# Splitting w_out on POOL, the first q and k on VectorE, and weight products placed sooner in a fused attention and expert kernel

## The chip, the cores and the metric

The kernel runs on one core of one Trainium2 chip. The metric is device time in microseconds (us), the median of several runs. TensorE is PE, its weight loads PEld, VectorE DVE, ScalarE ACT, GpSimd POOL; SP issues the DMAs.

## What is computed

Attention over 2 batches, 8 heads, 576 positions of width 64, mixed with a memory read; then a gated feed-forward block; then four experts. Cut to what matters:

```python
scores = scale * q @ k.T                 # causal mask, softmax -> a
local = a @ v
q_p = phi(q)                             # elu(q) + 1
mem_out = (q_p @ M_prev) / (q_p @ z_prev + 1e-6)
x = g * mem_out + (1 - g) * local        # 1152 tokens x 512
h = (x @ w1) * (x @ w2) @ w3             # w1, w2: 512 x 1024, w3: 1024 x 1024
x = h @ w_out                            # w_out: 1024 x 512
out = sum_e p[:, e] * (relu(x @ e_w1[e]) @ e_w2[e])   # four experts
```

The weights of the feed-forward block reach the chip as 64-bit floating-point numbers.

## The kernel before, in words

A product of two 32-bit numbers is made of three fast products: each operand is split into a high part (a copy rounded to the type `F32R`) and a low part (the operand less its high part), and the pairs in `PASSES` are summed. So each operand costs one instruction for its high part and one for its low part. `hi_pool` and `lo_pool` run on POOL, `nc.scalar.copy` makes a high part on ACT, `lo_dve` (line 82) a low part on DVE.

The feed-forward weights go through `from64` first: two ACT instructions (lines 101 and 102), then two on DVE (lines 103 and 106) put a 32-bit number together. Its temporary tiles `tf` and `tu` have two buffers each.

Attention works on pairs of heads, eight of them, in slots numbered -1 to 7. In slot n the pair n+2 is loaded and split (`stage_h`), the scores of pair n+1 are made (`stage_a`: products `sc`, a masked minimum by DVE at line 223 out of PSUM, an exponential by ACT at line 230), and pair n is transposed (`pt`, line 257), multiplied by v (`a`, line 270), joined with the memory read (`b`, line 294) and put into `xT`.

Between these steps stand the "fills", PE work that needs no attention result or an older one. `WO_SLOTS` says at which slot each of the eight blocks of w_out is split (`wo_unit`). `W_SLOTS` spreads 16 units that multiply w3 by w_out into `Wt` (`wacc`, line 380; their weights `w3s` are split by POOL). `B_SLOTS` spreads 16 units of x @ w1 and x @ w2 for the first half of the tokens (`ab`, line 432, weights `ws`). `C_SLOTS` spreads eight units of the product with `Wt` (`c`, line 493). The numbers only set the order in which the code is written; a scheduler then orders each engine's instructions. On the chip each engine runs its own list strictly in that order and waits on semaphores.

After attention come the second half of the tokens (again `ab` and `c`) and the experts (lines 600 and 617).

Of the kernel before, what the change touches and what calls it, by code (L numbers as in the profile page):

```python
# [21 lines left out]
T_AT = (0.01, 0.05, 0.09, 0.13, 0.17, 0.21, 0.25, 0.29)  # L22
MEM_AT, PV_AT, JOIN_AT, FIN_AT = 0.11, (0.4, 0.48), 0.54, 0.68

WO_SLOTS = (-0.9, -0.8, -0.7, -0.6, -0.3, -0.1, 0.1, 0.2)
W_SLOTS, B_SLOTS, C_SLOTS = (0.0, 4.0), (4.0, 6.4), (6.4, 8.0)

# [4 lines left out]
def kernel(  # L34
# [17 lines left out]
    nc = tc.nc  # L52
# [19 lines left out]
    def r32(ap):  # L72
        return ap.bitcast(F32)

    def hi_pool(dst, src):
        nc.gpsimd.tensor_scalar(out=dst, in0=src, scalar1=1.0, scalar2=1.0, op0=ALU.mult, op1=ALU.mult)  # L76

    def lo_pool(dst, src, hi):
        nc.gpsimd.tensor_sub(dst, src, r32(hi))  # L79

    def lo_dve(dst, src, hi):
        nc.vector.tensor_sub(dst, src, r32(hi))  # L82
# [10 lines left out]
    def from64(raw, tmp, nm):  # L93

        hi = raw[..., 1]
        shape = list(hi.shape)
        t = tmp.tile(shape, F32, tag="t64f", name=f"tf_{nm}")
        u = tmp.tile(shape, U32, tag="t64u", name=f"tu_{nm}")  # L100
        nc.scalar.activation(u, raw.bitcast(U16)[..., 1], AF.Copy, scale=2.0**-13, bias=2.0**-14 - 0.5)  # L101
        nc.scalar.activation(t, hi.bitcast(F32), AF.Copy, scale=2.0**-112)  # L102
        nc.vector.scalar_tensor_tensor(  # L103
            out=u, in0=t.bitcast(U32), scalar=3, in1=u, op0=ALU.logical_shift_left, op1=ALU.bitwise_or
        )
        nc.vector.scalar_tensor_tensor(  # L106
            out=t.bitcast(U32), in0=hi, scalar=0x80000000, in1=u, op0=ALU.bitwise_and, op1=ALU.bitwise_or
        )
        return t
# [47 lines left out]
    def stage_h(p):  # L157

        if p >= B * H // 2:
            return []  # L160
        qd, kd = raw_t[p]
        qk_t[p] = [A1.tile([P, 2, S], F32R, tag=f"{x}s", name=f"{x}s{p}") for x in "qk"]
        qs, ks = qk_t[p]
        return [
            *zip(
                H_AT,
                (
                    lambda: nc.scalar.copy(qs[:, 0, :], qd),
                    lambda: nc.scalar.copy(ks[:, 0, :], kd),
                    lambda: lo_pool(qs[:, 1, :], qd, qs[:, 0, :]),  # L170
                    lambda: lo_pool(ks[:, 1, :], kd, ks[:, 0, :]),
                ),
            )
        ]
# [149 lines left out]
    def run_slot(n, fill):  # L324
        steps = stage_h(n + 2) + stage_phi(n + 1) + stage_a(n + 1)
        steps += stage_b(n) if n >= 0 else []
        steps += [((i + 0.5) / len(fill), f) for i, f in enumerate(fill)]
        for _, f in sorted(steps, key=lambda t: t[0]):
            f()
# [5 lines left out]
    wo = [po.tile([P, 2, DM], F32R, tag=f"o{c}", name=f"wo{c}") for c in range(KF)]  # L335
# [10 lines left out]
    def wo_load(c):  # L346
        raw_o[c] = r = staging(f"wor{c}").rearrange("p a f two -> p (a f) two")
        nc.sync.dma_start(out=r.rearrange("p n two -> p (n two)"), in_=w_out[c * P : (c + 1) * P, :])

    def wo_unit(c):  # L350
        def f():
            if c + 3 < KF:
                wo_load(c + 3)
            f = from64(raw_o.pop(c), pf, f"wo{c}")
            nc.scalar.copy(wo[c][:, 0, :], f)
            lo_dve(wo[c][:, 1, :], f, wo[c][:, 0, :])
        return f

    NU = 2 * KF
# [28 lines left out]
    def w_unit(u):  # L388
        def pre():
            if u == 0:  # L390
                w_load(0), w_load(1), w_load(2), w_conv(0), w_conv(1)
            if u + 3 < NU:
                w_load(u + 3)

        def post():
            if u + 2 < NU:
                w_conv(u + 2)

        return [pre] + [lambda c=c: w_mm(u, c) for c in range(4)] + [post]
# [67 lines left out]
    for _, f in stage_h(0):  # L467
        f()
# [48 lines left out]
    def spread(slots, units):  # L517
        return [(slots[0] + (slots[1] - slots[0]) * i / len(units), u) for i, u in enumerate(units)]

    fills = [(at, [wo_unit(c)]) for c, at in enumerate(WO_SLOTS)]  # L520
    fills += spread(W_SLOTS, [w_unit(u) for u in range(NU)])
# [152 lines left out]
```

## Time and profile before

| | us |
|---|---|
| median of 3 runs (771.61 to 773.91) | 773.49 |
| the profiled execution | 772.15 |
| its span, first to last instruction | 770.4 |
| PE busy in the span | 743.0 (96%) |
| DVE, ACT, POOL busy | 299.5, 252.6, 246.1 |

A busy share says how long an engine had an instruction under way. PE is the engine that nearly fills the span, so the question for any edit is which of the 27 us in which PE has nothing under way it can give back, and whether PE's own instructions take the same time before and after. An instruction's idle time in front of it stands in square brackets with what released it.

### The profile page before, as it was taken

The numbers are of one execution on the slowest core, as the hardware profiler recorded it, in microseconds if no ns is written. First come the engines' busy times: TensorE is split into PE (matmuls) and PEld (weight loads), VectorE is DVE, ScalarE is ACT, GpSimd is POOL, SyncE is SP. The second block draws the span as 40 slices with busy tenths as digits, with TensorE's granted clock in tenths as the row PEclk, the third lists the DMA queues.
The fourth block names the chain that finished last, engine by engine and source line by source line (L and its number), as shares of the span: only waits on it lengthen the run. The fifth ranks groups of instructions, "written<-read, shape, count | busy, mean of one in ns | idle before, by whom it ended". The sixth has DMA issues, their size and how long they took to land.

```text
span 770.4 us, 11304 instructions
## 1 busy us (share of the span) xinstructions
PE 743.0 (96%) x4568; PEld 656.0 (85%) x4568; DVE 299.5 (39%) x642; ACT 252.6 (33%) x503; POOL 246.1 (32%) x244
## 2 busy tenths in 40 slices
PE   4899999999999998999999999999999999999997
PEld 2778888898888998999889898898988899888986
DVE  6967656667666225653312121212212122121221
ACT  7966556555556324542201011011111011010100
POOL 2164553444351029332940069000492003400000
PEclk9999999999999999999999999999999999999999
DMA  9773412332422015420420024000141000101010
GB/s 273 252 209 110 130 47 70 97 89 84 126 83 83 2 54 163 127 83 2 138 82 1 1 67 127 26 1 1 50 129 42 1 1 27 42 1 53 3 42 28
DMA packets 52596, 56.69 MB, mean 74 GB/s; under 512 B 15552, under 2 KB 40128, under 8 KB 52544
## 3 DMA queue, kind: packets, MB, share of 16 engines
q1 hardware_dynamic: 52544, 55.97, 24.1%
q8 instruction: 36, 0.59, 0.3%
q14 instruction: 16, 0.13, 0.1%
HBM read 53.60 MB, written 2.36 MB: 73 GB/s over the span
## 4 chain that ended last, share of the span: by engine, by line
PE 63%; DMA 2%; DVE 1%; POOL 1%; ACT 1%; issue 0%; DVEq 0%; SPq 0%; ACTq 0%
PE d L600 26%; PE o L617 26%; PE c L493 6%; PE ab L432 3%; DMA wr<-in_moe_w_dram 2%; PE a L270 1%; DVE tu L103 0%; POOL ws L79 0%; DVE tf L106 0%; PE pt L257 0%; POOL el L76 0%; POOL el L79 0%; DVE hT L82 0%; ACT tu L101 0%; ACT tf L102 0%
## 5 line engine op out<-in xcount | busy, mean ns | idle before, releaser
L617 PE MATMUL o<-el,he 128*128 128x512 f32 x864 | 201.3, 393 | 0.0
L617 PEld LDWEIGHTS o<-el,he 128*128 128x128 f32 x864 | 161.8, 188 | 36.6
L606 ACT ACTIVATE he<-d 128x512 fp32r<-128x512 f32 (+2 forms) x96 | 47.2, 491 | 342.4 <-PE d L600 339.9
L432 PE MATMUL ab<-xT,ws 128*128 128x288 f32 x768 | 113.1, 299 | 7.2 <-DVE asb L480 3.2
L600 PE MATMUL d<-x2b,el 128*128 128x384 f32 (+1 forms) x768 | 113.7, 308 | 0.0
L600 PEld LDWEIGHTS d<-x2b,el 128*128 128x128 f32 x768 | 113.1, 189 | 0.7
L432 PEld LDWEIGHTS ab<-xT,ws 128*128 128x128 f32 x768 | 103.9, 188 | 10.2 <-DVE asb L480 3.3
L607 DVE SCALAR_TENSOR_TENSOR he<-d,he 128x512 fp32r<-128x512 f32 (+2 forms) x96 | 53.5, 557 | 147.8 <-ACT he L606 147.8
L76 POOL TENSOR_SCALAR el<-rel 128x512 fp32r<-128x512 f32 x64 | 40.1, 632 | 216.3 <-PE d L600 187.2
L600 PE MATMUL d<-x2a,el 128*128 128x512 f32 x384 | 89.6, 394 | 0.0
L600 PEld LDWEIGHTS d<-x2a,el 128*128 128x128 f32 x384 | 72.0, 188 | 16.8
L79 POOL TENSOR_TENSOR el<-rel,el 128x512 fp32r<-128x512 f32 x64 | 83.1, 1313 | 1.6
L626 DVE SCALAR_TENSOR_TENSOR acc<-o,pr,acc 128x512 f32<-128x512 f32 x27 | 20.3, 751 | 125.7 <-PE o L617 125.7
L270 PEld LDWEIGHTS a<-v,pT 114*120 114x120 f32 (+1 forms) x480 | 55.4, 193 | 3.9 <-issue 2.6
L493 PE MATMUL c<-hT,W 128*128 128x288 f32 x384 | 57.6, 299 | 1.0 <-DVE hT L82 0.8
L270 PE MATMUL a<-v,pT 114*120 114x65 f32 (+1 forms) x480 | 56.7, 276 | 0.4 <-DVE mn L223 0.4
L79 POOL TENSOR_TENSOR ws<-tf,ws 128x512 fp32r<-128x512 f32 x32 | 44.9, 1402 | 38.2 <-ACT ws L422 36.9
L493 PEld LDWEIGHTS c<-hT,W 128*128 128x128 f32 x384 | 52.3, 188 | 2.6 <-DVE hT L82 1.5
L380 PE MATMUL wacc<-wo,w3s 128*128 128x512 f32 x192 | 49.9, 408 | 0.0
L217 PE MATMUL sc<-ks,qs 64*120 64x120 f32 (+5 forms) x288 | 37.2, 375 | 12.5 <-POOL ks L79 9.3
L230 ACT ACTIVATE P<-P,mn 120x120 f32<-120x120 f32 (+3 forms) x80 | 42.4, 578 | 2.0 <-DVE mn L223 1.8
L380 PEld LDWEIGHTS wacc<-wo,w3s 128*128 128x128 f32 x192 | 35.9, 194 | 7.6 <-issue 0.7
(75 smaller groups left out, 634.9 us busy)
## 6 DMA issues: line engine op xcount, KB each, us to landing
wr<-in_moe_w_dram SPq DMA_DIRECT2D x32, 512.0 KB, 3.6
rel<-in_moe_w_dram SPq DMA_DIRECT2D x64, 256.0 KB, 2.7
w3r<-in_moe_w3T_dram SPq DMA_DIRECT2D x16, 512.0 KB, 3.9
wor<-in_moe_w_out_dram SPq DMA_DIRECT2D x8, 512.0 KB, 6.7
v<-in_v_dram SPq DMA_DIRECT2D x16, 150.0 KB, 4.0
qd<-in_qT_dram SPq DMA_DIRECT2D x8, 288.0 KB, 3.3
kd<-in_kT_dram SPq DMA_DIRECT2D x8, 288.0 KB, 3.5
out_dram<-acc SPq DMA_DIRECT2D x9, 256.0 KB, 2.0
```

The costliest lines, as they stand in the source:

```text
L76: nc.gpsimd.tensor_scalar(out=dst, in0=src, scalar1=1.0, scalar2=1.0, op0=ALU.mult, op1=ALU.mult)
L79: nc.gpsimd.tensor_sub(dst, src, r32(hi))
L217: nc.tensor.matmul(ps[x][:, c : c + k1 - k0], lhsT=qs[o, a, q0[i] : q0[i] + RP], rhs=ks[o, b, k0:k1], start=(m == 0), stop=(m == 2),)
L230: nc.scalar.activation(Pt[i], Pt[i], AF.Exp, bias=mn[:, i : i + 1], scale=-1.0)
L270: nc.tensor.matmul(st["a"][:, x, i, :], lhsT=pt[x, i, j][0 : rows[j]], rhs=vn[0 : rows[j], j, :], start=(j == 0), stop=(j == i),)
L380: nc.tensor.matmul(wacc[t], lhsT=w3s[u][:, a, c, :], rhs=wo[4 * g + c][:, bb, :], start=(g == 0 and c == 0 and x == 0), stop=(g == 1 and c ...
L432: nc.tensor.matmul(ps[:, 0:HS], lhsT=self.ws[u][:, wi, kk, :], rhs=xT[b, kk][:, xi, a * HS : (a + 1) * HS], start=(n == 0), stop=(n == 3 * ...
L493: nc.tensor.matmul(st["ps"][:, 0:HS], lhsT=Wt[kk][:, wi, d * P : (d + 1) * P], rhs=hT[kk][:, xi, a * HS : (a + 1) * HS], start=(kk == 0 an ...
L600: nc.tensor.matmul(ps, lhsT=ew1[m // 4 * 4 + kk][:, wi, m % 4 * P : (m % 4 + 1) * P], rhs=rhs[:, xi, :], start=(n == 0), stop=(n == 3 * KD ...
L606: nc.scalar.activation(ht[:, 0, :], ps, AF.Relu)
L607: nc.vector.scalar_tensor_tensor(out=ht[:, 1, :], in0=ps, scalar=0.0, in1=r32(ht[:, 0, :]), op0=ALU.max, op1=ALU.subtract,)
L617: nc.tensor.matmul(po, lhsT=hs[kk][:, xi, tt * P : (tt + 1) * P], rhs=ew2[kk][:, wi, :], start=(n == 0), stop=(n == 3 * KF - 1),)
```

## The change

It does three things. The high and low parts of the eight w_out blocks are made by POOL; before, ACT made the high and DVE the low part. The low parts of q and k of the first pair (only that pair) are made by DVE; before, by POOL. And the slots move: the w_out blocks now all lie in slot -1, the w3 units start 0.2 slots sooner, the first `ab` units 0.2 sooner and over 2.5 slots where there were 2.4, the `c` units 0.1 sooner and over 1.7.

```diff
-WO_SLOTS = (-0.9, -0.8, -0.7, -0.6, -0.3, -0.1, 0.1, 0.2)
-W_SLOTS, B_SLOTS, C_SLOTS = (0.0, 4.0), (4.0, 6.4), (6.4, 8.0)
+WO_SLOTS = (-0.95, -0.85, -0.75, -0.65, -0.5, -0.35, -0.2, -0.1)
+W_SLOTS, B_SLOTS, C_SLOTS = (-0.2, 3.8), (3.8, 6.3), (6.3, 8.0)
...
+        lo = lo_pool if p else lo_dve
...
-                    lambda: lo_pool(qs[:, 1, :], qd, qs[:, 0, :]),
-                    lambda: lo_pool(ks[:, 1, :], kd, ks[:, 0, :]),
+                    lambda: lo(qs[:, 1, :], qd, qs[:, 0, :]),
+                    lambda: lo(ks[:, 1, :], kd, ks[:, 0, :]),
...
-            nc.scalar.copy(wo[c][:, 0, :], f)
-            lo_dve(wo[c][:, 1, :], f, wo[c][:, 0, :])
+            hi_pool(wo[c][:, 0, :], f)
+            lo_pool(wo[c][:, 1, :], f, wo[c][:, 0, :])
```

POOL's list from its first split on, before (`qs` and `ks` are the split q and k, 138 and 139 the first pair, 154 and 155 the second; `w3s` is a split w3 unit):

```order
L79 TENSOR_TENSOR qs_138<-qd_122,qs_138 128x576
L79 TENSOR_TENSOR ks_139<-kd_124,ks_139 128x576
L79 TENSOR_TENSOR qs_154<-qd_148,qs_154 128x576
L79 TENSOR_TENSOR ks_155<-kd_150,ks_155 128x576
L76 TENSOR_SCALAR w3s_369<-tf_l_363 128x512
L79 TENSOR_TENSOR w3s_369<-tf_l_363,w3s_369 128x512
```

The same place now (`wo_114` is the first split w_out block, `wo_121`, further down, the last):

```order
L76 TENSOR_SCALAR wo_114<-tf_wo_172 128x512
L79 TENSOR_TENSOR wo_114<-tf_wo_172,wo_114 128x512
L76 TENSOR_SCALAR wo_115<-tf_wo_182 128x512
L79 TENSOR_TENSOR wo_115<-tf_wo_182,wo_115 128x512
L76 TENSOR_SCALAR wo_116<-tf_wo_192 128x512
L79 TENSOR_TENSOR wo_116<-tf_wo_192,wo_116 128x512
L76 TENSOR_SCALAR wo_117<-tf_wo_223 128x512
L79 TENSOR_TENSOR wo_117<-tf_wo_223,wo_117 128x512
L79 TENSOR_TENSOR qs_154<-qd_148,qs_154 128x576
L79 TENSOR_TENSOR ks_155<-kd_150,ks_155 128x576
```

Four w_out blocks stand ahead of the second pair's q and k, and the other four between these and the first w3 unit: 16 POOL instructions more in front of the first `w3s`.

DVE's list from its third instruction on, before:

```order
L188 TENSOR_SCALAR ex_156<-ex_156 128x576
L189 SCALAR_TENSOR_TENSOR phi_157<-qd_122,ex_156 128x576
L103 SCALAR_TENSOR_TENSOR tu_wo_173<-tf_wo_172,tu_wo_173 128x512
L106 SCALAR_TENSOR_TENSOR tf_wo_172<-wor_130,tu_wo_173 128x512
L103 SCALAR_TENSOR_TENSOR tu_wo_204<-tf_wo_203,tu_wo_204 128x512
L82 TENSOR_TENSOR wo_114<-tf_wo_172,wo_114 128x512
L106 SCALAR_TENSOR_TENSOR tf_wo_203<-wor_132,tu_wo_204 128x512
```

And now:

```order
L82 TENSOR_TENSOR qs_138<-qd_122,qs_138 128x576
L189 TENSOR_SCALAR ex_156<-ex_156 128x576
L82 TENSOR_TENSOR ks_139<-kd_124,ks_139 128x576
L190 SCALAR_TENSOR_TENSOR phi_157<-qd_122,ex_156 128x576
L103 SCALAR_TENSOR_TENSOR tu_wo_173<-tf_wo_172,tu_wo_173 128x512
L106 SCALAR_TENSOR_TENSOR tf_wo_172<-wor_130,tu_wo_173 128x512
L103 SCALAR_TENSOR_TENSOR tu_wo_183<-tf_wo_182,tu_wo_183 128x512
```

The low parts of the first q and k have come in, and the low part of the first w_out block is gone (so are the other seven further down).

POOL's list early in the second half of the tokens, before (`el` is a split expert weight, `ws_2` the third split unit of w1 and w2 of that half):

```order
L76 TENSOR_SCALAR el_0_1_3873<-rel_0_1_3871 128x512
L76 TENSOR_SCALAR el_0_2_3878<-rel_0_2_3876 128x512
L79 TENSOR_TENSOR el_0_1_3873<-rel_0_1_3871,el_0_1_3873 128x512
L79 TENSOR_TENSOR el_0_2_3878<-rel_0_2_3876,el_0_2_3878 128x512
L79 TENSOR_TENSOR ws_2_3261<-tf_2_3255,ws_2_3261 128x512
```

And now:

```order
L76 TENSOR_SCALAR el_0_1_3873<-rel_0_1_3871 128x512
L76 TENSOR_SCALAR el_0_2_3878<-rel_0_2_3876 128x512
L79 TENSOR_TENSOR el_0_1_3873<-rel_0_1_3871,el_0_1_3873 128x512
L79 TENSOR_TENSOR ws_2_3261<-tf_2_3255,ws_2_3261 128x512
L79 TENSOR_TENSOR el_0_2_3878<-rel_0_2_3876,el_0_2_3878 128x512
```

The low part of `ws_2` has changed places with that of an expert weight.

## Rows read from the trace of the kernel before

**Rows 1.** Stretches: start:end, length, busy PE, PEld, DVE, ACT, POOL, clock, DMA

```profile
8.61:40.12 31.51, 25.80 (x145) 20.81 (x145) 30.18 (x82) 28.79 (x56) 4.98 (x4) 1.00 0.89 269
...
146.00:250.00 104.00, 98.83 (x810) 91.39 (x809) 68.59 (x167) 61.15 (x127) 41.35 (x37) 1.00 0.31 93
284.00:360.00 76.00, 72.34 (x529) 70.25 (x528) 38.36 (x60) 34.89 (x72) 36.35 (x30) 1.00 0.34 104
```

**Rows 2.** Timeline, first microseconds: start us, us, engine line op tiles [idle before]

```profile
5.98 0.66 ACT L169 CAST ks<-kd 128x576 fp32r<-128x576 f32 x1
...
6.93 1.62 POOL L79 TENSOR_TENSOR ks<-kd,ks 128x576 fp32r<-128x576 f32 x1
...
7.32 1.85 DVE L189 SCALAR_TENSOR_TENSOR phi<-qd,ex 128x576 f32<-128x576 f32 x1
...
8.61 2.88 PE L217 MATMUL sc<-ks,qs 64*120 64x120 f32 x24 [8.61 <-POOL ks L79]
```

**Rows 3.** Timeline of PE, around its first products with weights

```profile
33.28 4.66 PE L270 MATMUL a<-v,pT 114*120 114x65 f32 x22 [0.41 <-DVE mn L223]
...
40.12 0.77 PE L380 MATMUL wacc<-wo,w3s 128*128 128x512 f32 x1
...
42.26 4.17 PE L380 MATMUL wacc<-wo,w3s 128*128 128x512 f32 x12
...
54.88 5.72 PE L380 MATMUL wacc<-wo,w3s 128*128 128x512 f32 x24
```

**Rows 4.** Timeline of DVE and POOL, the last steps before the first weight product

```profile
37.04 0.68 DVE L106 SCALAR_TENSOR_TENSOR tf_l<-w3r,tu_l 128x512 uint32<-128x512 uint32 x1
...
38.51 1.58 POOL L79 TENSOR_TENSOR w3s<-tf_l,w3s 128x512 fp32r<-128x512 f32 x1
```

**Rows 5.** Groups of DVE, 10 to 38 us: count | busy us, mean ns | idle before

```profile
L82 DVE TENSOR_TENSOR wo<-tf_wo,wo 128x512 fp32r<-128x512 f32 x8 | 6.9, 860 | 0.5 <-ACT wo L355 0.4
L106 DVE SCALAR_TENSOR_TENSOR tf_wo<-wor,tu_wo 128x512 uint32<-128x512 uint32 x8 | 5.5, 685 | 0.1
L103 DVE SCALAR_TENSOR_TENSOR tu_wo<-tf_wo,tu_wo 128x512 uint32<-128x512 uint32 x7 | 4.8, 681 | 0.0
```

**Rows 6.** Groups of POOL, 36 to 75 us

```profile
L79 POOL TENSOR_TENSOR w3s<-tf_l,w3s 128x512 fp32r<-128x512 f32 x8 | 11.2, 1398 | 0.7
L76 POOL TENSOR_SCALAR w3s<-tf_l 128x512 fp32r<-128x512 f32 x8 | 5.5, 683 | 28.4 <-DVE tf_l L106 15.6 <-PE wacc L380 12.8
```

**Rows 7.** Timeline, DVE instructions that meet a POOL instruction

```profile
22.20 1.41 POOL L79 TENSOR_TENSOR ks<-kd,ks 128x576 fp32r<-128x576 f32 x1
...
22.33 1.82 DVE L82 TENSOR_TENSOR wo<-tf_wo,wo 128x512 fp32r<-128x512 f32 x1 [0.17 <-ACT wo L355]
...
47.00 1.30 POOL L79 TENSOR_TENSOR w3s<-tf_l,w3s 128x512 fp32r<-128x512 f32 x1
...
47.13 0.75 DVE L223 CUSTOM_DVE_ANT_0 P<-sc,mask,mn 120x512 f32<-120x512 f32 x1 [0.77 <-PE sc L217]
```

**Rows 8.** Groups of DVE, 38 to 110 us, where POOL splits w3 units

```profile
L103 DVE SCALAR_TENSOR_TENSOR tu_l<-tf_l,tu_l 128x512 uint32<-128x512 uint32 x13 | 11.5, 887 | 12.4 <-ACT tf_l L102 12.4
L106 DVE SCALAR_TENSOR_TENSOR tf_l<-w3r,tu_l 128x512 uint32<-128x512 uint32 x13 | 10.0, 771 | 0.8
...
L82 DVE TENSOR_TENSOR xT<-x,xT 128x576 fp32r<-128x576 f32 x2 | 1.5, 744 | 0.0
```

**Rows 9.** Timeline, two of PE's later waits and what stands before them

```profile
212.39 1.82 PE L432 MATMUL ab<-xT,ws 128*128 128x288 f32 x12 [1.95 <-POOL ks L79]
...
289.70 0.62 ACT L422 CAST ws<-tf 128x512 fp32r<-128x512 f32 x1 [0.60 <-PE ab L432]
...
290.73 1.54 POOL L79 TENSOR_TENSOR ws<-tf,ws 128x512 fp32r<-128x512 f32 x1
...
292.32 3.19 PE L432 MATMUL ab<-xT,ws 128*128 128x288 f32 x22 [1.71 <-POOL ws L79]
```

## The prediction, made before the changed kernel ran

> **What bounds the kernel now.** I read the busy time by stretch first and looked for PE's idle time. It has nothing under way for 8.61 us until its first product [rows 2], for 31.51 - 25.80 = 5.71 us from there to its first weight product at 40.12, for 104.00 - 98.83 = 5.17 between 146 and 250, and for 76.00 - 72.34 = 3.66 between 284 and 360 [rows 1]. With the last 4 us, in which DVE and a DMA finish after PE, that is all of the 27 us. From 360 on there is nothing that the change could hide better.
>
> Next I read how fast PE runs. The clock column says 1.00 in all these stretches, so I go by durations: 22 `a` products take 4.66 us at 33.28; 12 `wacc` products 4.17 us at 42.26, but 24 of the same only 5.72 us (0.238 each) at 54.88 [rows 3]. If the slow ones take twice that, 4.17 us are some 5.5 slow ones and 6.5 fast ones, which puts the change of pace at 42.26 + 2.6 = 44.9. So PE runs at its lower level, 1.2 GHz, for the first 45 us and at 2.4 GHz after. What stands ahead of the first weight product, 25.80 us of work, is done at the low level in both kernels, and what counts is when the weight products can start. I call that moment T; before, T = 40.12.
>
> What sets T is DVE. In 8.61 to 40.12 it is busy for 30.18 of 31.51 us, POOL for 4.98 [rows 1]. DVE's line 106 ends the first w3 unit at 37.72, POOL's low part of it ends at 40.09, and PE's first `wacc` starts at 40.12 [rows 3, 4].
>
> **Part by part.** *First q and k.* POOL's low part of k ends at 8.55 and PE starts at 8.61; ACT had its high part ready at 6.64 [rows 2]. DVE needs 0.74 us for one of that size [rows 8]: q at 5.6, ex at 6.3, k from 6.72 to 7.47, so PE starts at 7.5, 1.1 us sooner. phi, which took 1.85 us beside POOL's work and ended at 9.17 [rows 2], then takes 0.74 too and ends at 8.2, so DVE reaches the w_out blocks 0.9 us sooner. This is worth something only if DVE keeps its lead until T.
>
> *What leaves DVE and ACT.* Eight copies leave ACT, and eight low parts, 6.9 us in sum [rows 5], leave DVE; seven of these (some 5.9 us) stand in front of the first w3 unit. With DVE's list otherwise the same, line 106 would end at 37.72 - 0.9 - 5.9 = 30.9 and T be 33.3. PE can't be ready sooner either: 7.5 + 25.8 = 33.3. That is the best case.
>
> *What comes to POOL.* Eight times 0.68 + 1.40 us [rows 6], 16.6 us, with the second pair's q and k (2 x 1.4, [rows 7]) in the middle. From 9.6 on this ends at 29.0 if POOL never waits, so POOL's length alone isn't the bound. But DVE waits for POOL. The low part at 22.33 took 1.82 us where line 103 of like size takes 0.68, and it ended 0.54 us after POOL's instruction of 22.20 had ended; the minimum out of PSUM at 47.13 met a POOL instruction as well and took 0.75, no more than the 0.74 above [rows 5, 7, 8]. So a DVE instruction with both inputs in SBUF doesn't run beside one of POOL's, and one out of PSUM does. The Trainium skill, page "SBUF — State Buffer", section "Who interferes with whom", says the same: DVE with two SBUF inputs and a POOL instruction that reads SBUF shut each other out, and whoever comes second waits. By that rule the best case can't be had, and offering work to POOL isn't free.
>
> The price of that. DVE has 21 such instructions between 9.5 us and the end of line 106 for the first w3 unit (8 of line 103, 8 of 106, 3 of ex, 2 of phi). From below: where POOL splits w3 units now, line 103 takes 0.21 us more than here and line 106 0.09 [rows 5, 8]; 0.15 each for 21 is 3.1, so T = 36.4. From above: I walked DVE's and POOL's new lists side by side from 8.2 us, with these durations, DVE's PSUM work (5 us a pair) running beside POOL, and each clash going to whoever was there first. Twelve waits come out, 0.1 to 1.2 us, 7.6 in sum; the largest lie behind the second pair's q and k (1.2), the sixth block (1.1) and the eighth (0.8). DVE also waits a little for ACT, which can't refill a temporary tile before POOL has read it. Line 106 then ends at 39.6, and POOL, held up by DVE in turn, ends the first unit at 42.4. I take T = 41, nearer the walk, since in the stretch of rows 8 POOL rests about half the time, and here it has a queue.
>
> *From T on.* All of the first head's `a` products now stand ahead of T (0.45 us of them came after it), so the end moves by 41 - 40.12 - 0.45 = +0.4. The pace changed 4.8 us after T, with the same work in between; I keep that, with 2 us either way, worth 1 us, since work at the low level takes twice as long. The second block of `wacc` needs two units that POOL makes behind the third pair's q and k: in the walk they are there at 54.3 and needed at 56, so this costs nothing; with POOL 2 us later it would cost 0.5.
>
> *Slots.* Between 45 and 146 us PE is full already, so products that come sooner find no idle time there. In 146 to 250 the 5.17 us are mostly waits of `ab` for a PSUM buffer that ACT or DVE empties late; the largest is 1.95 at 212.39 [rows 9]. It is put down to POOL's split of k, which these products don't read; the copies they need stood on ACT behind q, k and two exponentials. The new list spreads the 16 units over 4% more time and gives each such place other neighbours. A gain or loss of up to 2 us is open; I take 0. SP's list changes by one or two places, with loads of w3 and w1 ahead of a q or k that they followed; I cost that at nothing, since the loads run ahead of their use by a slot.
>
> *After attention.* PE waits 1.71 us at 292.32 for a low part that POOL began at 290.73, behind expert weights; its high part was ready at 290.32 [rows 9]. With the two changed about it can start 0.4 us sooner: -0.4.
>
> **Sum.** On the profiled execution 772.15 + 0.4 + 0 - 0.4 = 772.2. The median of the runs lies 1.34 above that execution, so 773.5.
>
> **Rivals.** *DVE and POOL seldom meet.* With T = 37 the end moves by -3.6 - 0.4: 769.5. For it: the small excess of rows 8. Against: POOL's queue is full here. Chance 0.25.
>
> *DVE waits as in the walk, and longer (the side of slower).* The place is DVE's list between 20 and 42 us. Each wait there also holds up the minimum behind it, for which PE's next scores wait, and line 106, for which POOL's next block waits. It decides from T = 43 on, where the shift is +2.4; at 43.7, with 0.5 at the second block of `wacc`, it gives 776.7. Chance 0.22.
>
> *The slots decide.* If the new neighbours clear the 5.17 us [rows 1] the time is 768.3, if they add half as much 776.1; 0.04 each.
>
> *The clock comes sooner.* PE had hardly a gap from 33.7 to 44.9 and stayed at the low level until the `wacc` stream [rows 3], so the rows speak against it. The work between T and the change of pace, 4.8 us, done at the high level gives back 2.4: 771.1, on the edge of no change; 0.03. The Trainium skill, page "TensorE: Matmul & The Clock Gate", says in its first part that the low clock is the default and sustained activity releases it. The trace bears that out for the `wacc` stream, and not for the small products ahead of it.
>
> **Numbers.** A measurement of this kernel can tell 0.3%, 2.3 us, from no change. No change has 0.45 (the forecast 0.42, the sooner clock 0.03); faster 0.25 + 0.04; slower 0.22 + 0.04. T from 36.4 to 44.5 with the slots' 2 us and the clock's 1 us reaches from 766 to 781; without the outer fifth, 768.5 to 778.
>
> **What would show it.** In the new profile: PE's first product near 7.5; DVE's lines 103 and 106 before 40 us at 0.9 to 1.1 us in the mean (0.68 if they don't meet POOL); the first `wacc` near 41 with PE idle for some 4 us in front of it; the change of pace 3 to 7 us later; 3 to 7 us of waits between 146 and 250; the wait near 292 at 1.3. The forecast is wrong if T lies below 38.5 or above 43, or if the stretch 146 to 250 gains or loses more than 2 us.

## The result, and the profile after

| | median us | runs |
|---|---|---|
| before | 772.07 | 6 (771.38 to 773.91) |
| changed | 778.74 | 6 (777.63 to 780.79) |

The ratio is 1.0086, 95% interval 1.007 to 1.0102: the change makes the kernel slower by 6.7 us. The forecast was no change, 773.5 us in a range of 768.5 to 778. The profiled execution of the changed kernel took 777.63 us, 5.48 more than that of before.

From line 164 on every line number is one higher than before (one line was added). The stretches of the changed kernel, to hold against [rows 1] (columns as there):

```profile
7.49:40.61 33.12, 23.77 (x147) 18.62 (x147) 30.98 (x73) 27.48 (x52) 22.01 (x19) 0.94 0.89 271
40.61:61.00 20.39, 16.86 (x75) 13.31 (x76) 11.70 (x20) 9.99 (x16) 10.80 (x10) 0.76 0.57 164
...
286.00:364.00 78.00, 73.17 (x536) 70.92 (x535) 41.92 (x60) 36.51 (x77) 37.50 (x30) 1.00 0.33 105
```

PE has nothing under way for 33.12 - 23.77 = 9.35 us between its first product and its first weight product, where it was 5.71, and for another 3.53 us in the 20 us behind it. The clock column (1.00 is 2.4 GHz, 0.50 is 1.2 GHz) needs care: ahead of the first rise in the records it shows 1.00 for the lower level too. So in [rows 1] it said 1.00 for a stretch that ran at 1.2 GHz; here it is under 1 because the clock rose at 29.7 us, fell at 36.5, rose at 46.8, fell at 57.0 and rose for good at 60.4. Before, it rose once, at 44.7.

The timeline of PE in the changed kernel, its larger waits up to 60 us (start, length, instruction, idle time ahead and what ended it), to hold against [rows 2, 3]:

```profile
7.49 2.88 PE L218 MATMUL sc<-ks,qs 64*120 64x120 f32 x24 [7.49 <-DVE ks L82]
...
25.68 1.55 PE L218 MATMUL sc<-ks,qs 64*120 64x120 f32 x12 [1.67 <-POOL ks L79]
...
34.58 4.51 PE L271 MATMUL a<-v,pT 114*120 114x65 f32 x30 [2.74 <-DVE mn L224]
40.61 0.79 PE L381 MATMUL wacc<-wo,w3s 128*128 128x512 f32 x1 [1.52 <-POOL w3s L76]
...
53.21 0.78 PE L258 MATMUL pt<-identF,P 120*120 120x120 f32 x6
57.52 0.77 PE L381 MATMUL wacc<-wo,w3s 128*128 128x512 f32 x1 [3.53 <-DVE W L82]
```

The first product stands at 7.49 and the first weight product at 40.61, where the forecast had 7.5 and 41. The last line is new: the second block of `wacc` waits 3.53 us. It is released by VectorE's low part of `W`, which is made out of the accumulator of the first block. That accumulator is the same PSUM buffer (tag M1, one buffer), so no product of the second block can start before `W` has been made from it, although the first block's last product ended at 50.5.

Why `W` came so late stands in the timelines of POOL, ACT and DVE of the changed kernel (in this order, not by time):

```profile
49.58 1.42 POOL L79 TENSOR_TENSOR qs<-qd,qs 128x576 fp32r<-128x576 f32 x1 [3.56 <-ACT qs L169]
50.95 1.41 POOL L79 TENSOR_TENSOR ks<-kd,ks 128x576 fp32r<-128x576 f32 x1
52.32 0.62 POOL L76 TENSOR_SCALAR w3s<-tf_l 128x512 fp32r<-128x512 f32 x1
53.03 1.27 POOL L79 TENSOR_TENSOR w3s<-tf_l,w3s 128x512 fp32r<-128x512 f32 x1
54.27 0.62 POOL L76 TENSOR_SCALAR w3s<-tf_l 128x512 fp32r<-128x512 f32 x1
54.97 1.26 POOL L79 TENSOR_TENSOR w3s<-tf_l,w3s 128x512 fp32r<-128x512 f32 x1
...
54.33 0.67 ACT L102 ACTIVATE tf_l<-w3r 128x512 f32<-128x512 f32 x1 [2.91 <-POOL w3s L79]
54.91 0.57 ACT L386 CAST W<-wacc 128x512 fp32r<-128x512 f32 x1
...
55.03 1.75 DVE L103 SCALAR_TENSOR_TENSOR tu_l<-tf_l,tu_l 128x512 uint32<-128x512 uint32 x1 [5.46 <-ACT tf_l L102]
56.70 0.68 DVE L82 TENSOR_TENSOR W<-wacc,W 128x512 fp32r<-128x512 f32 x1
```

Read it from the end. VectorE's `W` stands behind line 103, which took 1.75 us beside POOL's instruction of 54.97 (it ended 0.55 us after it) and had waited 5.46 us for ACT. ACT's copy of the accumulator stands behind line 102, which waited 2.91 us for a temporary tile `tf` (two buffers) to be read by POOL. POOL read it last at 53.03, because ahead of it stood q and k of the third pair, and POOL sat idle for 3.56 us until ACT had made their high parts. Nobody here needed q and k of the third pair yet (PE's first scores from them start at 73.24); they only stood in the list. Before, POOL's third unit of w3 stood ahead of them, at 47.00 [rows 7].

To account for the whole 5.48 us I add up PE's time in the two traces: its first product -1.12; waits from there to 64 us +6.87 (6.02 to 12.89); waits from 64 to 284 us -2.83 (5.17 to 2.34); waits behind that +1.17 (3.66 to 4.83); the products themselves +1.39 (743.05 to 744.43). The products can be split further. PE's busy time at the lower level (before the first rise, and wherever the records say 0.5) was 30.43 us and is 28.77. My estimate is that half of it would go at the upper level; that is 15.2 and 14.4 us, so 0.8 came back there, and the rest of the busy time grew by 2.2 us, from 727.8 to 730.0.

### The profile page after: what moved, and what is told of

It is laid out like the page before. It is cut to its first block, busy times and chain, and to the rows that moved or that the text cites. A ratio compares the mean times of both kernels' runs of the same rounds, so it can differ in the third digit from the quotient of the medians.

```text
span 775.8 us, 11324 instructions
## 1 busy us (share of the span) xinstructions
PE 744.4 (96%) x4568; PEld 655.3 (84%) x4568; DVE 300.5 (39%) x636; ACT 252.3 (33%) x495; POOL 263.7 (34%) x258
## 4 chain that ended last, share of the span: by engine, by line
PE 62%; DMA 3%; POOL 2%; DVE 2%; ACT 2%; issue 1%; DVEq 0%; POOLq 0%; SPq 0%; ACTq 0%
PE d L601 26%; PE o L618 26%; PE c L494 5%; PE ab L433 3%; DMA wr<-in_moe_w_dram 3%; PE a L271 2%; POOL el L79 1%; POOL ws L79 1%; DVE tf L106 1%; POOL el L76 1%; PE pt L258 1%; ACT tu L101 1%; PE sc L218 0%; DVE tu L103 0%; ACT tf L102 0%
## 5 line engine op out<-in xcount | busy, mean ns | idle before, releaser
L381 PE MATMUL wacc<-wo,w3s 128*128 128x512 f32 x192 | 54.5, 426 | 5.5 <-DVE W L82 4.0
L271 PEld LDWEIGHTS a<-v,pT 114*120 114x120 f32 (+1 forms) x480 | 53.7, 188 | 5.2 <-DVE mn L224 3.0
L271 PE MATMUL a<-v,pT 114*120 114x65 f32 (+1 forms) x480 | 54.6, 270 | 2.7 <-DVE mn L224 2.7
L381 PEld LDWEIGHTS wacc<-wo,w3s 128*128 128x128 f32 x192 | 36.8, 201 | 14.9 <-issue 5.9
```

What stands on the lines that cost most here:

```text
L271: nc.tensor.matmul(st["a"][:, x, i, :], lhsT=pt[x, i, j][0 : rows[j]], rhs=vn[0 : rows[j], j, :], start=(j == 0), stop=(j == i),)
L381: nc.tensor.matmul(wacc[t], lhsT=w3s[u][:, a, c, :], rhs=wo[4 * g + c][:, bb, :], start=(g == 0 and c == 0 and x == 0), stop=(g == 1 and c ...
```

## The experiments

The change has three parts: **S**, the slots; **O**, w_out on POOL; **Q**, the first pair's q and k on VectorE. All eight settings were run, and then variants. Each time is a median, with the kernel before run on the same chip in the same job. The columns after the ratio come from each kernel's profiled execution, by the sum above: first product, waits to 64, from 64 to 284 and behind 284 us, half of the busy time at the lower level (an estimate of what that level costs), and all other busy time.

| run | what it has | median, before | ratio (95%) | first | waits | half low | other |
|---|---|---|---|---|---|---|---|
| before | | | | 8.61 | 6.0, 5.2, 3.7 | 15.2 | 727.8 |
| the change | S O Q | 778.74, 772.07 | 1.007 to 1.010 | 7.49 | 12.9, 2.3, 4.8 | 14.4 | 730.0 |
| after_again | S O Q | 780.84, 771.95 | 1.0075 to 1.013 | 7.41 | 11.4, 4.5, 4.1 | 18.7 | 729.9 |
| slots_only | S | 771.16, 771.64 | 0.998 to 1.001 | 8.58 | 7.7, 2.1, 4.4 | 12.7 | 730.0 |
| wo_pool_only | O | 774.86, 771.64 | 1.002 to 1.005 | 8.56 | 8.5, 3.4, 4.1 | 15.6 | 728.5 |
| qk_dve_only | Q | 771.89, 771.64 | 0.999 to 1.002 | 7.47 | 7.7, 3.9, 2.9 | 16.5 | 727.0 |
| slots_qk | S Q | 776.09, 771.64 | 1.004 to 1.008 | 7.47 | 5.8, 3.7, 4.4 | 18.6 | 729.4 |
| slots_wo | S O | 778.61, 771.95 | 1.005 to 1.010 | 8.57 | 10.2, 3.2, 4.5 | 14.9 | 730.9 |
| qk_wo | O Q | 778.36, 771.95 | 1.005 to 1.009 | 7.48 | 13.0, 3.5, 3.9 | 17.4 | 727.5 |

The change and after_again are the same kernel, and their profiled executions differ by 1.5, 2.2 and 0.7 us in the three columns of waits and by 4.3 us in the lower level. So one execution's difference of that size says little by itself.

**The slots alone** (slots_only). Edit:

```diff
-WO_SLOTS = (-0.9, -0.8, -0.7, -0.6, -0.3, -0.1, 0.1, 0.2)
-W_SLOTS, B_SLOTS, C_SLOTS = (0.0, 4.0), (4.0, 6.4), (6.4, 8.0)
+WO_SLOTS = (-0.95, -0.85, -0.75, -0.65, -0.5, -0.35, -0.2, -0.1)
+W_SLOTS, B_SLOTS, C_SLOTS = (-0.2, 3.8), (3.8, 6.3), (6.3, 8.0)
```

> The kernel before with only the three rows of slots changed (w_out's units and the products with weights 0.2 of a pair sooner); w_out's parts stay on ScalarE and VectorE, the first pair's low parts of q and k on GpSimd. Theory A (the loss comes from w_out's parts on GpSimd, which make GpSimd late and hold up ScalarE): no wait of more than 1 us ahead of the second block of products w3 with w_out; the waits between 146 and 250 us fall from 5.2 to about 1.3 us, the ones after 284 us grow by 1.2 us: 772.1 - 3.9 + 1.2, so 769.4 us, 768 to 771. Rival B (the slots themselves put the second block too soon after the first): a wait of 3 to 4 us ahead of the second block here too, and a time of 776 to 778.5 us.

Measured 771.16 us, no difference from before and just above theory A's bracket. The second block waited 1.87 us, between the two theories. The waits between 64 and 284 us did fall by 3.1 us, yet the time did not, and the trace says where that went. One line each for before, this kernel and the one with w_out on POOL alone, from the end of the second `wacc` block to the same product `c` at the end of attention (the 192nd), columns as in [rows 1]:

```profile
60.60:283.00 222.40, 217.22 (x1730) 195.90 (x1729) 131.78 (x337) 122.10 (x245) 83.05 (x73) 1.00 0.27 78
```

```profile
59.53:280.87 221.34, 219.34 (x1738) 197.02 (x1736) 128.41 (x336) 124.55 (x243) 84.56 (x73) 1.00 0.27 79
```

```profile
64.17:284.78 220.61, 217.18 (x1730) 195.89 (x1729) 130.03 (x337) 122.68 (x245) 82.65 (x73) 1.00 0.27 78
```

With the old slots PE is busy 217.2 us there, with the new ones 219.3 (220.2 in the changed kernel). Seven more transposes lie in the stretch, 0.6 us; the other 1.5 is the same products at the same clock. This is no chance of one execution: cut in the same way, qk_dve_only, qk_wo and before_qkall, with the old slots, lie within 0.1 us of before, and the other kernels with the new ones and no added products have 3.0 to 4.5 us more than before (in slots_qk and slots_wo the clock fell once in the stretch). Counted in the traces, `wacc` products and attention's change places more often (165 changes from one kind of product to another became 178), and a block that is broken up takes longer: before, 24 `wacc` in a row took 5.72 us [rows 3], 15 and 9 of them 3.68 + 2.31. So the new slots fill PE's waits, and PE's own products take back most of what that gives. That the finer mixing is the reason fits these counts; no run tested it alone.

**w_out on POOL alone** (wo_pool_only). Edit:

```diff
-            nc.scalar.copy(wo[c][:, 0, :], f)
-            lo_dve(wo[c][:, 1, :], f, wo[c][:, 0, :])
+            hi_pool(wo[c][:, 0, :], f)
+            lo_pool(wo[c][:, 1, :], f, wo[c][:, 0, :])
```

> The kernel before with only w_out's high and low parts moved to GpSimd; slots and q, k as before. Theory A: the second block of products w3 with w_out waits 2 to 5 us, for an accumulator that is emptied late or for a part of w_out, TensorE's clock comes later or falls once more, and nothing is given back between 146 and 250 us (5.2 us of waits as before): 777 to 782 us, above the changed kernel's 778.7 more likely than below. Rival B: within 1.5 us of the kernel before, 771 to 773.5 us, since the slots stand as before.

Measured 774.86 us, 3.2 above before: under theory A's bracket and over rival B's. No wait stood ahead of its second block; it lost 2.5 us in waits before 64 us, one of them for q and k of the second pair behind w_out on POOL (2.79 us at 28.0).

**The first q and k alone** (qk_dve_only). Edit:

```diff
+        lo = lo_pool if p else lo_dve
...
-                    lambda: lo_pool(qs[:, 1, :], qd, qs[:, 0, :]),
-                    lambda: lo_pool(ks[:, 1, :], kd, ks[:, 0, :]),
+                    lambda: lo(qs[:, 1, :], qd, qs[:, 0, :]),
+                    lambda: lo(ks[:, 1, :], kd, ks[:, 0, :]),
```

> The kernel before with only the first pair's low parts of q and k moved from GpSimd to VectorE. Both theories: the first product comes 1.1 us sooner (near 7.5 us), the start of the products with weights is set by VectorE and not by q and k, so at most this 1.1 us is kept and at worst VectorE is as much later: 771 to 772.8 us, waits after 61 us as before.

Measured 771.89 us, as expected. The first product came 1.1 us sooner and nothing of it was left.

**Slots with q and k** (slots_qk; the first and third edit).

> The changed kernel with w_out's parts put back on ScalarE and VectorE: slots and the first pair's q and k as changed. Theory A: 768 to 771 us, faster than the kernel before, no wait over 1 us ahead of the second block, and about 1.3 us of waits between 146 and 250 us. Rival B: the wait of 3 to 4 us ahead of the second block stays, 775 to 778.5 us. Rival C (the fallen clock is the loss, and the wait only its sign): the clock is granted in full from the first block on in this kernel if its products run without a wait, and the 24 products of the second block take 5.7 us rather than 7.1.

Measured 776.09 us. Theory A fails here: with w_out off POOL the kernel is still 4.5 us slower than before, though no wait over 0.45 us stands between 33 and 87 us. Rival B has the time but not its wait. What the trace shows instead is the clock. The same 22 `a` products in slots_only and in slots_qk, on PE's timeline:

```profile
33.26 2.52 PE L270 MATMUL a<-v,pT 114*120 114x65 f32 x22 [0.51 <-DVE mn L223]
```

```profile
33.07 4.66 PE L271 MATMUL a<-v,pT 114*120 114x65 f32 x22 [0.45 <-DVE mn L224]
```

In slots_only the clock had risen at 32.5 us (it fell again at 35.9 and rose for good at 42.8); in slots_qk it rose at 47.0. In the table that is 18.6 against 12.7 us, more than the whole difference of the two profiled executions (775.04 and 771.20). Part of it comes much later: PE waited 1.92 us for VectorE ahead of 183.53, the clock was lower from 183.6 to 187.0, and 12 `ab` products took 3.24 us there where the next 12 took 1.85. Of rival C's sign half is there, without a gain: the second block's 24 products take 5.73 us, but the first block began at the lower level. All 9 runs of slots_qk (774.0 to 778.3) lie above all 12 of slots_only (770.0 to 773.0), but a clock record exists for one execution of each, so that the clock explains all the runs is not shown.

**The two other pairs** (slots_wo, qk_wo; the first and second, the second and third edit), with the change once more beside them (after_again).

> The changed kernel as it is, once more, on the chip of the next three: 777.5 to 779.5 us, with about 3.5 us of wait ahead of the second block of products w3 with w_out, behind GpSimd, ScalarE and VectorE in this order.

> The changed kernel with the first pair's low parts of q and k back on GpSimd: slots and w_out as changed. By the sum of the parts measured alone (slots -0.5 us, w_out on GpSimd +3.2 us) 774.3 us. Theory A (w_out on GpSimd and the sooner slots together make the wait ahead of the second block): 776 to 779 us, with 3 us or more of wait there. Rival D (the sooner q and k together with the slots are what costs, 4.7 us more in that pair than the two alone): 773.5 to 775 us.

> The changed kernel with the slots back as before: w_out on GpSimd and the first pair's q and k on VectorE. By the sum of the parts measured alone (+3.2 and +0.25 us) 775.1 us; theories A and D both 774 to 776 us, with less than 1.5 us of wait ahead of the second block and 3.4 us or more of waits between 61 and 284 us. Above 777 us, neither holds: q and k with w_out would then be a pair that costs by itself.

The change measured 780.84 us, above its bracket, with 4.22 us of wait ahead of the second block. slots_wo had theory A's time, 778.61, without its wait: its waits stand ahead of the first block, and its second block runs at 57.3 without one. Two of them on PE's timeline, for POOL and for VectorE:

```profile
28.04 1.55 PE L217 MATMUL sc<-ks,qs 64*120 64x120 f32 x12 [2.79 <-POOL ks L79]
...
36.47 1.68 PE L270 MATMUL a<-v,pT 114*120 114x65 f32 x14 [1.85 <-DVE mn L223]
```

qk_wo, 778.36, lies above what either theory allowed, and with the old slots shows the chain of the changed kernel once more. From its timelines of ACT, DVE and PE:

```profile
54.23 0.67 ACT L102 ACTIVATE tf_l<-w3r 128x512 f32<-128x512 f32 x1 [2.91 <-POOL w3s L79]
...
58.81 0.68 DVE L82 TENSOR_TENSOR W<-wacc,W 128x512 fp32r<-128x512 f32 x1
...
59.14 1.65 PE L258 MATMUL pt<-identF,P 120*120 120x120 f32 x7 [5.88 <-ACT pT L260]
```

So that chain doesn't need the new slots. ACT waits 2.91 us for POOL as in the changed kernel, and PE 5.88 us for a copy that ACT makes behind it.

Over the eight settings w_out on POOL costs 3.2 us (old slots, old q and k), 7.1 (new slots), 6.2 (new q and k), and 2.2 to 4.4 (both; by the two jobs that ran the change). It is the one part that costs in every setting. The three don't add. From the first weight product to the end of the second block of `wacc` the four kernels with w_out on POOL take 22.2 to 27.9 us, before 20.5, and the other three settings 19.2 to 21.9. But only the change and qk_wo show the chain of ACT's 2.91 us there; what w_out on POOL costs in wo_pool_only and slots_wo is not explained by it.

**The cause taken away** (after_p2dve). The changed kernel with q and k of the third pair on VectorE, which stood idle for 5.46 us just there. The lists of ACT and PE stay as they are:

```diff
-        lo = lo_pool if p else lo_dve
+        lo = lo_dve if p in (0, 2) else lo_pool
```

> The changed kernel with one more edit: the low parts of q and k of the third pair are made by VectorE too, which stood idle from 49.6 to 55.0 us, and no longer by GpSimd ahead of the third and fourth unit of w3. The orders of ScalarE and of TensorE stay as they are. Theory A (the accumulator of the second block is emptied late because ScalarE and VectorE stand behind GpSimd's q and k of the third pair): GpSimd's third unit ends near 48 instead of 54.3 us, the accumulator is empty near 53.5 instead of 57.4 us, the wait of 3.5 us ahead of the second block falls under 0.6 us, the clock does not fall there, and the time comes down by 3 to 5 us, to 774 to 776 us. Rival E (the clock and the finer mixing of products are the loss, the wait is made up later): less than 1 us is gained, 778 to 779 us.

Measured 775.67 us against 780.84 for the change in the same job: 5.2 us gained, and inside theory A's 774 to 776. (The change had only 4 runs there. By the first measurement, 6.7 us over before against 3.7 here, it is 3.0.) The same places in its timelines (POOL, ACT, DVE, PE):

```profile
49.47 1.30 POOL L79 TENSOR_TENSOR w3s<-tf_l,w3s 128x512 fp32r<-128x512 f32 x1
...
52.56 0.59 ACT L386 CAST W<-wacc 128x512 fp32r<-128x512 f32 x1
...
50.22 1.16 DVE L82 TENSOR_TENSOR qs<-qd,qs 128x576 fp32r<-128x576 f32 x1
51.30 0.75 DVE L82 TENSOR_TENSOR ks<-kd,ks 128x576 fp32r<-128x576 f32 x1
...
54.36 0.68 DVE L82 TENSOR_TENSOR W<-wacc,W 128x512 fp32r<-128x512 f32 x1
...
55.18 1.17 PE L381 MATMUL wacc<-wo,w3s 128*128 128x512 f32 x4 [0.35 <-DVE W L82]
```

POOL's third unit of w3 ends at 50.8 instead of 54.3, ACT's line 102 waits for nothing, and the wait ahead of the second block is 0.35 us. The clock rose for good at 47.9 and didn't fall again. From the first weight product to the end of the second block, where the edit acts, this kernel takes 19.6 us, the change 24.0 (24.9 in after_again) and before 20.5. The sum of waits to 64 us shows less of it (11.4 to 10.0), because in this execution more wait, 9.7 us for 7.1, stood ahead of that product. 3.7 us over before remain. By the sum they are wait ahead of the first weight product (9.7 us, before 5.7) and other busy time (+2.7), less what the lower level costs (-2.3).

**All q and k on VectorE** (before_qkall, slots_qkall, after_qkall: the kernel before, slots_qk and the change, with `lo = lo_dve` for every pair).

> The kernel before with the low parts of q and k of all eight pairs made by VectorE (14 more than in the run with the first pair alone): GpSimd is rid of 16 subtractions of 1.4 us, VectorE gets 16 of 0.7 us, 11 us over some 250. Theory A (GpSimd's queue is what holds the others up): the waits that end with GpSimd's ks, 0.7 us at 23.7 and 1.9 us at 212.4, go, and the time falls to 768.5 to 771 us. Rival F (VectorE is as full as GpSimd and its row minima and the experts' sums come later instead): 772 to 776 us, with as much wait named by VectorE.

> Slots as changed, w_out on ScalarE and VectorE as before, low parts of q and k of all pairs on VectorE. The same with the first pair alone took 776.1 us. Theory A: GpSimd's queue is 20 us shorter, the wait of 1.9 us near 183.5 us that ends with VectorE's asb, whose operations there take 1.3 to 1.75 us beside GpSimd, falls under 1 us and the clock does not fall there: 771 to 774.5 us. Rival F: 776 to 779 us.

> The changed kernel with the low parts of q and k of all pairs on VectorE; with the first and third pair there it took 775.7 us. Theory A: no wait over 0.6 us ahead of the second block, the waits of 1.7 us at 25.7 us (for GpSimd's ks of the second pair) gone, 772 to 775.5 us. Rival F: VectorE's row minima come later ahead of 40 us, where it is busy 31 of 33 us: 776 to 779 us.

Measured 770.65 (before 772.13, ratio 0.9972 to 1.0001), 773.74 and 773.09 us. All three lie inside theory A's brackets, but the first is at the edge of what can be told from no change, and its mechanism was only half right: the wait of [rows 9] at 212.39 is now 1.73 us at 210.66 and ends with a copy by ACT, as the prediction had read it: POOL's k had not been its cause.

**Products that nobody reads** (p2_warm, then after_warm, p2_warm_early, after_qkall_warm). To see whether the falling clock is a loss of its own, products of 128x512 were added for some blocks `c` of w_out, two each, into a PSUM bank that is free then; on after_p2dve, on the change, and on after_qkall:

```diff
+            if c >= 4:
+                ps = psM.tile([P, 512], F32, tag="M0", name=f"warm{c}", bufs=1)
+                for i in range(2):
+                    nc.tensor.matmul(ps, lhsT=wo[c][:, 0, 0:P], rhs=wo[c][:, 0, :], start=(i == 0), stop=(i == 1))
```

In p2_warm_early the condition is `c < 4`.

> The changed kernel with q and k of the third pair on VectorE (775.7 us), and with eight products of 128x512 that nobody reads, two for each of the last four parts of w_out, placed ahead of 40 us, where TensorE waits 2.6 and 1.9 us; each takes 0.43 us at the lower clock. Theory C (the clock that falls in these waits is a loss of its own): the clock stays at the upper level from about 31 us on, the first block of 24 products w3 with w_out takes some 6 instead of 7.7 us, 772.5 to 775 us. Rival G (the added products lie ahead of attention's and delay it by up to 3.4 us, and the clock falls all the same): 776 to 779 us.

> The changed kernel with the eight added products of 128x512 that nobody reads (two for each of the last four parts of w_out), and q and k of the third pair on GpSimd as it was. Theory A with C (two losses that add): the wait of 3.5 us or more ahead of the second block stays, since GpSimd's queue is as long as it was, and the clock falls there; the clock is at the upper level when the first block runs: 775 to 777.5 us. Rival H (the clock alone is the loss, the wait is only seen because of it): under 773.5 us.

> As the kernel with q and k of the third pair on VectorE and eight added products (771.2 us), but these belong to the first four parts of w_out and so run between 11 and 28 us, ahead of the waits near 35 and 41 us. Theory C (what helps is wide products where TensorE would wait, just ahead of the first block): the two waits stay and the clock falls in them, 775 to 777.5 us, no better than without them (775.7). Rival I (any added products help, by the order that they bring): 771 to 773 us.

> The changed kernel with q and k of all pairs on VectorE (773.1 us) and the eight added products ahead of 40 us. Theory C: the waits of 1.8 us at 36.4 and 1.0 us at 39.7 are filled, the clock is at the upper level when the first block begins, 769 to 771.5 us. Rival G (the added products only delay attention): 773 to 775 us.

| run | without, with the added products | first | waits | half low | other |
|---|---|---|---|---|---|
| after_p2dve | 775.67 | 8.04 | 10.0, 3.3, 5.4 | 13.0 | 730.5 |
| p2_warm | 775.67, 771.19 | 7.49 | 6.8, 0.9, 5.8 | 12.1 | 732.4 |
| p2_warm_early | 775.67, 770.31 | 7.47 | 6.4, 2.1, 5.6 | 8.9 | 733.0 |
| after_warm | 780.84, 775.11 | 7.95 | 7.7, 2.4, 4.7 | 15.6 | 732.4 |
| after_qkall_warm | 773.09, 773.66 | 7.44 | 7.7, 3.3, 4.4 | 11.6 | 733.9 |

The medians of a pair come from different jobs, whose kernels before lie within 0.35 us of each other. Eight useless products make two of the three base kernels 4.5 to 5.7 us faster (after_warm only 3.4, if each kernel is held against its own before and the change is taken from its first measurement). p2_warm lies under theory C's bracket, p2_warm_early under both of its brackets. In p2_warm they run where PE had waited, and the first block then runs at the upper level at once (PE's timeline):

```profile
36.10 0.71 PE L361 MATMUL warm<-wo 128*128 128x512 f32 x2
...
41.38 1.22 PE L361 MATMUL warm<-wo 128*128 128x512 f32 x2
...
44.34 0.48 PE L385 MATMUL wacc<-wo,w3s 128*128 128x512 f32 x1
```

One `wacc` product takes 0.48 us there; in the changed kernel it took 0.79. So the mechanism of theory C happens, but the table says that it is not the larger part in p2_warm: the lower level's cost falls by 0.9 us, while the waits fall by 3.3 and 2.4 and the other busy time, the added products among it, grows by 1.9; with these products in between, the scheduler's order changes too. That the clock gave the gain there is thus not shown. In p2_warm_early, which by theory C should have gained nothing, the lower level's cost falls by 4.1 us (the clock was up from 16.1 to 22.9 and from 33.2 on): there the clock is the largest single term (the waits fall by 3.6 and 1.2), and my expectation of where the products have to stand was wrong. after_warm has the time expected but not the wait: its first block began 5 us later (45.5), and its second at 59.9 without one. after_qkall_warm gained nothing: the clock was up from 29.3 us on, as theory C wanted, and then PE waited for POOL and it fell at 49.8:

```profile
50.84 1.22 PE L314 MATMUL x<-identF,xq 114*128 114x114 f32 x5 [3.11 <-POOL xq L303]
```

**A version that beats both** (before_qkall_warm, before_warm, before_qkall_warm_early). The kernel before with q and k of all pairs on VectorE and two added products for w_out's blocks 3 to 5; the same without the first; the same with blocks 0 to 2.

> The kernel before with q and k of all pairs on VectorE (770.7 us) and six added products of 128x512, two for each of w_out's parts 3 to 5, w_out itself on ScalarE and VectorE. TensorE hardly waits there between 28 and 54 us, so the six cost 1.3 us at the upper or 2.6 us at the lower clock, and what they can bring is the clock some 3 to 10 us sooner than at 47.7 us, 1.5 to 5 us of products: theory C 768 to 770.5 us; rival G 771.5 to 774 us.

> The kernel before with only the six added products of 128x512 for w_out's parts 3 to 5. If the clock was a loss of the kernel before too, and apart from GpSimd's queue: 3 us faster, as the pair with q and k of all pairs on VectorE was (770.65 to 767.57), so 768 to 769.5 us. If the two only help together: 771 to 773 us.

> The kernel before with q and k of all pairs on VectorE and six added products for w_out's parts 0 to 2, among the first pair's work. If what counts is that wide products come early, as the changed kernel with early ones (770.3 against 771.2 us) lets one think: 765.5 to 768 us. If the place just ahead of the first block counts: 770 to 772.5 us, the clock up early and down again in a wait ahead of 28 us.

Measured 767.57 us (before 771.80, ratio 0.9915 to 0.9956), 771.99 (before 770.96, 0.9988 to 1.0027) and 769.32 (before 770.96, 0.9949 to 0.999). The first is faster than both kernels, by 0.6% than before and by 1.4% or more than the change; it lies just under theory C's bracket, and the third between its two. Neither half does it alone. Why it is faster isn't shown: its profiled execution (770.08) is one of its slowest, and differs from that of before_qkall (770.76) by 1.3 us less wait between 64 and 284 us and 0.6 us more of other busy time, while the lower level costs 18.0 against 17.6 us.

## Why the prediction was wrong, by its own steps

- **First product and T: right, T in part by luck.** 7.49 for 7.5, 40.61 for 41, with 2.74 + 1.52 = 4.3 us of wait ahead, for some 4. The walk along the lists of VectorE and POOL was near: VectorE's line 106 ended at 39.85 (39.6 in the walk), POOL's first unit at 41.92 (42.4). But T doesn't hang on the end of that unit, as I had read. The first product reads only the high part. Before, that was there at 38.43, and PE came to it at 40.12 out of its own list, with no idle time ahead [rows 3]; now PE waits for it, and the low part ends 1.3 us after T. POOL before, then POOL in the changed kernel:

```profile
37.81 0.62 POOL L76 TENSOR_SCALAR w3s<-tf_l 128x512 fp32r<-128x512 f32 x1 [14.20 <-DVE tf_l L106]
```

```profile
39.94 0.62 POOL L76 TENSOR_SCALAR w3s<-tf_l 128x512 fp32r<-128x512 f32 x1 [0.63 <-DVE tf_l L106]
40.64 1.28 POOL L79 TENSOR_TENSOR w3s<-tf_l,w3s 128x512 fp32r<-128x512 f32 x1
```

  So 41, a middle between 36.4 and 42.4, fits for another reason than the one given. The walk's price shows in the groups of DVE, 10 to 38 us, where [rows 5] had 681 and 685:

```profile
L103 DVE SCALAR_TENSOR_TENSOR tu_wo<-tf_wo,tu_wo 128x512 uint32<-128x512 uint32 x7 | 7.6, 1080 | 0.2 <-ACT tf_wo L102 0.2
...
L106 DVE SCALAR_TENSOR_TENSOR tf_wo<-wor,tu_wo 128x512 uint32<-128x512 uint32 x7 | 6.8, 972 | 0.3
```

  The three `ex` that I counted with them have one input, not two; they too took longer, 609 ns for 450 in the mean.

- **"The second block ... costs nothing; with POOL 2 us later it would cost 0.5": the step that failed.** It measured 3.5 us (4.2 in after_again), and the clock that fell in the wait made the block's 24 products take 7.10 us where they took 5.72 before: 4.9 us in all. Taking the cause of the wait away gave 3.0 to 5.2. The block in the changed kernel, then in after_p2dve:

```profile
57.52 7.10 PE L381 MATMUL wacc<-wo,w3s 128*128 128x512 f32 x24 [3.53 <-DVE W L82]
```

```profile
55.18 5.74 PE L381 MATMUL wacc<-wo,w3s 128*128 128x512 f32 x24 [0.35 <-DVE W L82]
```

  Of the two units that I had put at 54.3, the third ended at 54.3 and the fourth at 56.2; but PE was there at 54.0, not 56. Above all, the step looked only at the weights. The block also needs its accumulator, and the copy that empties it stood on ACT and VectorE behind work for units that nobody needed yet, which waited for POOL through the two `tf` buffers. The prediction named that link ("ACT, which can't refill a temporary tile before POOL has read it") and followed it up to T only.
- **The pace of PE: right in its first step, wrong after it.** The clock rose 6.2 us behind T, inside the 3 to 7 us. That it had already risen at 29.7 and fallen, and that a wait of 3.5 us would bring it down again at 57.0, was no term of the sum. In the profiled execution of the change this didn't cost more than before did (14.4 against 15.2 us); in after_again it did (18.7).
- **Slots, 0 with 2 us either way: right in the sum, wrong inside.** The waits between 146 and 250 us fell from 5.2 to 1.2 us (3.4 in after_again), more than the 2 us that I had named as a sign of being wrong. Up to the end of attention they fell by 2.8 us, and PE's own products took as much longer between the same two points (217.2 to 220.2 us, some 0.8 of it transposes that moved in). slots_only, with a ratio of 0.9996, shows the same without w_out.
- **After attention, -0.4: wrong, +1.2** (+0.4 in after_again). slots_only has +0.7, wo_pool_only +0.4 and qk_dve_only -0.7; two executions of the change differ as much, so which part it belongs to is not shown. In the changed kernel and in slots_only the wait for POOL's low part moved and stayed 1.51 us, and sums of VectorE that `c` needs are now waited for:

```profile
316.10 1.71 PE L433 MATMUL ab<-xT,ws 128*128 128x288 f32 x11 [1.51 <-POOL ws L79]
```

- **The rivals.** "DVE waits as in the walk, and longer" had the sign and almost the time (776.7), but not the mechanism: T didn't pass 43. None of the rivals put its loss behind T, where the only price in the whole sum was 0.5; so the range ended at 778.0.

## What to carry to other kernels

When work moves to an engine with room, follow its list past the point where it is first needed: each wait that it sends to another engine also holds what stands behind it there, and a copy that empties an accumulator is needed as much as the data of the next products. Idle time that was filled by other places for the products was paid for here in the products; compare PE's busy time between the same two products, not its waits alone. Parts of a change that measure nothing alone (slots -0.5 us, q and k +0.2) cost 4.5 us together here, so measure the pairs.

## What the runs showed of the hardware that I had not expected

- The granted clock rose and fell with small things, mostly in the first 60 us, but also at 183.6 in slots_qk and at 301.3 in after_again. In or just behind waits of PE of 2.1 to 5.9 us it fell from 2.4 to 1.2 GHz in the changed kernel (at 36.5 and 57.0), in qk_wo (at 34.5 and 58.4) and in after_qkall_warm (at 49.8). The Trainium skill, page "TensorE: Matmul & The Clock Gate", first part, ties the level to how busy PE has lately been, and these falls agree. What no run here gives is a rule by which the moment could be told: in slots_only it fell at 35.9, where the only wait over 0.1 us since it rose at 32.5 was one of 0.51, and in slots_qk PE had no wait over 0.05 us between 33.5 and 47 and was at the lower level all that time.
- Products that nobody reads made two kernels faster, by 3.4 to 5.7 us, though two of them take 0.7 to 1.2 us of PE.
- One VectorE instruction of 128x512 with both inputs in SBUF took 1.75 us beside POOL where the next one of line 103 took 0.68, and it stood in front of the copy that PE waited for. The mean of 1.08 us between 10 and 38 us doesn't show such a case.
